# Third pair's second product by Strassen's scheme, with the weight sums made in place and the first product's weight sums read back from DRAM

## The chip, the cores and the metric

The kernel runs on one core of one Trainium2 chip. The metric is the device time of one launch in microseconds (us), lower is better. TensorE is called PE (matmuls) and PEld (weight loads), VectorE is DVE, ScalarE is ACT, GpSimd is POOL, SyncE is SP.

## The reference

Attention without softmax, and then a feed-forward block with a residual, for 8 batches of 448 rows, 12 heads of 64 columns (d_model 768), and d_ff 3072:

```python
scores = (q @ k.T) / sqrt(64)                 # per batch and head, 448 x 448
x = (maximum(scores, 0) ** 2 / 448) @ v       # heads side by side: 448 x 768
xn = (x - mean(x)) / sqrt(var(x) + 1e-6) * g_ln
out = x + maximum(xn @ w_ch1, 0) @ w_ch2      # 768 -> 3072 -> 768
```

The arrays are float32 in DRAM; the kernel multiplies in bfloat16 and sums in float32.

## The kernel before

**Pairs and stages.** The kernel works on pairs of batches: pair p holds batches 2p and 2p + 1, 896 rows. `xT[p]` is the attention's output with its columns on the partitions, `hT[p]` the hidden layer (24 row blocks of 128 x 896), `xtok[p]` the attention's output with tokens on the partitions, made from `xT[p]` by a DMA transpose (`tokens`). Pair 0 runs first, its pieces interleaved. After that, pairs are staggered, and each pass of the loop `for pair in range(pairs - 1)` runs two stages:

- A0, A1, A2: the second product (`hT[p]` times `w2`, L693) of pair 0, 1, 2, interleaved with the attention of the next pair (`attention`, L336 for scores, L368 for values).
- F1, F2, F3: the first product (`xT` times `w1`) of pair 1, 2, 3, in `ffn1_pair`.

The last part of the kernel is the second product of pair 3, with nothing beside it.

**Order.** The schedule is manual: each engine runs its instructions in the order in which the Python code issues them, and waits on semaphores for data or for a buffer to be free. Nothing reorders them. `interleave` spreads a list of side units evenly among a list of main units.

**Attention beside the second product.** A pair's attention has six groups of heads, n = 6p to 6p + 5, each with seven score tiles (128 x 896: two PSUM banks, three such tiles in turn, shared with the value product). Three score tiles form a bundle: 12 matmuls, three relus on ACT (L347), three squares on DVE (L351; in A0 the third on ACT, L349). Some bundles also hold a value product (28 matmuls, `product`), whose result DVE scales into `xT` (L374). A2 has 14 bundles, two hooks and a last value product: 17 side units. Keys and queries are loaded by POOL (`load`) and transposed by DMAs that SP issues (`transposed`, three groups ahead).

**The ordinary second product.** `ffn2` computes 128 tokens x 384 columns in 24 matmuls, in four units of six; two PSUM banks (`ps_mm`) alternate. DVE's L704 scales the result, adds the residual and so empties the bank. 14 such results make a pair: 336 matmuls. Rows 11 and 23 of `hT` come last (`late_rows`), because the last step of the stage before (`close`) makes them.

**Strassen's scheme for the first product.** `ffn1_pair` splits `w1` into four blocks, and the batch pair into two. For each of 12 iterations n it makes seven products of three matmuls instead of eight, on sums of blocks: products 3, 4, 1, then `close` of the iteration before (7 and 6), then 5 and 2. DVE adds the results: `z += b` (L863), `z += c` (L865), `a = z - a` (L877), `b = z - b` (L880). Product 2 accumulates into bank b, so it can't start before L863 has read that bank. The sums of `w1` blocks are made by POOL and DVE, in F2 they are also stored to `kept` in DRAM (`keep`, 44 stores on SP), and in F3 they are read from there (`given`). The sums of `xT` halves (L738) are made in `even`, `odd` and `start`.

**Strassen's scheme for the last pair's second product.** `ffn2_pair` takes token tiles t and t + 4 together (t = 0, 1, 2) and both column halves, four results, with seven products of 12 matmuls, 84 instead of 96. The left sides are sums of `hT` blocks (s1, s2, s5, s6, s7; `h_sums_of`, L942 to L948), the right sides blocks of `w2` (t2, t5) or their sums (t1, t3, t4, t6, t7). POOL makes t3, t4, t1 and t6 in F3 (48 instructions, L923), DVE t7 after it, all into buffers of their own. In the four results, `d`, `c12`, `c21` and `q_` are float32 buffers in SBUF; ACT copies banks into them, DVE and POOL add them up. Token tile 3 is left to `ffn2`.

Of the kernel before, what the change touches and what calls it, by code (L numbers as in the profile page):

```python
# [28 lines left out]
def kernel(  # L29
# [54 lines left out]
    xcpool = ctx.enter_context(tc.tile_pool(name="xc", bufs=2))  # L84
    xtpool = ctx.enter_context(tc.tile_pool(name="xt", bufs=1))
    hpool = ctx.enter_context(tc.tile_pool(name="h", bufs=1))
    opool = ctx.enter_context(tc.tile_pool(name="o", bufs=3))
# [8 lines left out]
    eps_sb = const.tile([P, 1], fp32)  # L96
    nc.vector.memset(eps_sb, 1e-6)
    ones = const.tile([P, P], bf16)
    nc.vector.memset(ones, 1.0)


# [16 lines left out]
    def load(n, names):  # L118
        if n >= len(groups):
            return  # L120
        b, m = groups[n]
        for name in names:
            if b == 1 and name != "v":
                o = (2 * m + "qk".index(name)) * 2 * S
                t = hold[:, o:o + 2 * S].rearrange("p (r s) -> p r s", r=2)
            elif name == "q":
                t = qbuf[m][:, D:D + 2 * S].rearrange("p (r s) -> p r s", r=2)
            else:
                t = io.tile([P, 2, S], bf16, tag=name, name=name + "_sb", bufs=4 if name == "v" else 3)
            nc.gpsimd.dma_start(t, srcs[name][b][:, m:NP:G, :])  # L130
            qkv[name, b, m] = t
# [34 lines left out]
    qkv["k", 0, 0] = io.tile([P, 2, S], bf16, tag="k", name="k_sb", bufs=3)  # L166
# [62 lines left out]
    def transposes(b, m):  # L229
# [8 lines left out]
        else:  # L238
            sb = tpool.tile([P, NB, P], bf16, tag="qT", name="qT_sb", bufs=3)
# [41 lines left out]
    def keys_dma(n):  # L281
        kts[n] = tpool.tile([P, J, P], bf16, tag="kT", name="kT_sb", bufs=3)
        nc.sync.dma_start_transpose(kts[n], qkv[("k",) + groups[n]].rearrange("p r s -> p (r s)"))

    def queries_dma(n):
        m, kt = groups[n][1], kts[n]
        qt = tpool.tile([P, NB, P], bf16, tag="qT", name="qT_sb", bufs=3)
# [69 lines left out]
    def values(n, blk):  # L357
# [21 lines left out]
        if b not in xc:  # L379
            xc[b] = xcpool.tile([P, K1, S + 2], bf16, tag="xc", name="xc_sb")  # L380
# [35 lines left out]
    def fold_tiles():  # L416

        t = xcpool.tile([P, K1, S + 2], bf16, tag="xc", name="fold_sb").rearrange("p c s -> p (c s)")
# [54 lines left out]
    def transposed(n):  # L473
# [6 lines left out]
        if n > by_dma * G:  # L480
            load(n + 2, "kq")
        keys_dma(n)
        queries_dma(n)

# [77 lines left out]
    def attention(bs, hooks):  # L562
# [9 lines left out]
        def item(n, i, act):  # L572
            scores(n, (i,), FULL, act)
            if i == J - 1 and n + 3 < len(groups):
                transposed(n + 3)

        def product(n):
            values(n, FULL)
            load(n + 4, "v")
# [120 lines left out]
    def finish(pair, t, half, lo, hi, ps, queues):  # L700

        cols, w = slice(half * DH + lo * D, half * DH + hi * D), (hi - lo) * D
        o = opool.tile([P, DH], fp32, tag="o", name="o_sb")
# [18 lines left out]
    def ffn1_pair(pair, keep=False, prepare=None, between=None):  # L722
# [6 lines left out]
        xd = xcpool.tile([P, K1, S + 2], bf16, tag="xc", name="x_sum")[:, :, :S]  # L729
# [3 lines left out]
        rooms[0] = {m: room0[:, a:b] for m, (a, b) in kinds.items()}  # L733
        given = prepare is not None

        def x_sum(m, a, b, op):
            if given:
# [9 lines left out]
        def sums_early(n):  # L747
# [5 lines left out]
            if given:  # L753
                queue = nc.scalar if n > 2 else nc.sync
                queue.dma_start(w[n]["early"], kept[:, n, :3 * KQ])
# [8 lines left out]
        def sums_late(n):  # L764
            if n >= KH:
                return
            if given:
                nc.sync.dma_start(w[n]["late"], kept[:, n, 3 * KQ:])
# [43 lines left out]
        def even():  # L812
            if given:
                rooms[0].update(early=room0[:, :3 * KQ], late=room0[:, 3 * KQ:])
            sums_early(0)
            nc.vector.tensor_add(x[5], lo[:, :KQ], lo[:, KQ:])
            sums_late(0)
            sums_last(0)

        def odd():  # L820
            nc.vector.tensor_sub(x[6], hi[:, :KQ], lo[:, :KQ])

        def start():
            z = xcpool.tile([P, K1, S + 2], bf16, tag="xc", name="z_sb").rearrange("p c s -> p (c s)")
            temps.extend(z[:, i * S2:(i + 1) * S2].bitcast(fp32) for i in range(2))
            if given:
                room, pool = prepare()
                for i, m in enumerate((1, 2, 7)):
                    x[m] = room[:, i * KQ * S:(i + 1) * KQ * S].rearrange("p (c s) -> p c s", s=S)
                for i in range(1, 3):  # L830
                    t = pool.tile([P, 5 * KQ, P], bf16, name=f"w1_room{i}")
                    rooms[i] = {m: t[:, a:b] for m, (a, b) in kinds.items()}
                    rooms[i].update(early=t[:, :3 * KQ], late=t[:, 3 * KQ:])
                for n in (1, 2):
                    sums_early(n)
                    sums_late(n)
            else:
# [3 lines left out]
                for i in range(1, 3):  # L841
                    one, two = (apool.tile([P, 2, 512], bf16, tag="attn", name="w1_sum")
                                .rearrange("p r (c n) -> p (r c) n", n=P) for _ in range(2))
                    rooms[i] = {3: two[:, :3], "4a": one[:, 6:8], "4b": two[:, 6],
                                4: (None, one[:, 6], one[:, 7], two[:, 6]),
                                1: one[:, :3], 6: one[:, 3:6], 7: two[:, 3:6], "16": one[:, :6]}
            x_sum(1, lo[:, :KQ], hi[:, KQ:], nc.vector.tensor_add)
            x_sum(2, hi[:, :KQ], hi[:, KQ:], nc.vector.tensor_add)
            x_sum(7, lo[:, KQ:], hi[:, KQ:], nc.vector.tensor_sub)
            if not given:  # L850
# [41 lines left out]
    w2_sum, h_sum, h_sums = {}, {}, (("s2", "s5"), ("s1",), ("s6",), ("s7",))  # L892
# [5 lines left out]
    def late_pools():  # L898

        late = ctx.enter_context(tc.tile_pool(name="late", bufs=1, side="right"))  # L900
        for name in ("t1", "t3", "t4", "t6"):
            w2_sum[name] = late.tile([P, KH, DH], bf16, name="w2_sum_" + name)
        w2_sum["t2"], w2_sum["t5"] = w2_part(0, 0), w2_part(1, 1)
        last = stage_sums.enter_context(tc.tile_pool(name="x_sums", bufs=1, side="right"))
        w1_pool = stage_sums.enter_context(tc.tile_pool(name="w1_kept", bufs=1, side="right"))
        return last.tile([P, KH * DH], bf16, name="x_sum"), w1_pool

    def late_pools_two():

        two = ctx.enter_context(tc.tile_pool(name="late2", bufs=1, side="right"))  # L910
        w2_sum["t7"] = two.tile([P, KH, DH], bf16, name="w2_sum_t7")
        return two

    def w2_sum_units():

        b = {(i, j): w2_part(i, j) for i in range(2) for j in range(2)}
        pairs = (("t3", (0, 1), (1, 1)), ("t4", (1, 0), (0, 0)), ("t1", (0, 0), (1, 1)),
                 ("t6", (0, 0), (0, 1)), ("t7", (1, 0), (1, 1)))

        def unit(name, x, y, i, n):  # L920
            engine = nc.vector if name == "t7" else nc.gpsimd
            op = engine.tensor_sub if name in ("t3", "t4") else engine.tensor_add
            op(w2_sum[name][:, i:i + n], b[x][:, i:i + n], b[y][:, i:i + n])  # L923
        return [lambda name=name, x=x, y=y, i=i, n=n: unit(name, x, y, i, n)
                for name, x, y in pairs for n in ((3,) if name == "t7" else (1,)) for i in range(0, KH, n)]

    def h_sum_tiles():

        three = xpool.tile([P, 3, KH, P], bf16, tag="xT", name="h_sum")
        h_sum["s2"], h_sum["s5"], h_sum["s1"] = (three[:, i] for i in range(3))  # L930
        h_sum["s25"] = three[:, 0:2]
        for name in ("s6", "s7"):
            t = xcpool.tile([P, K1, S + 2], bf16, tag="xc", name="h_sum1").rearrange("p c s -> p (c s)")
            h_sum[name] = t[:, :KH * P].rearrange("p (k s) -> p k s", s=P)

    def h_sums_of(pair, t, names, lo, hi):
# [300 lines left out]
```

## Time and profile before

| | us |
|---|---|
| median of three runs | 521.63 |
| profiled execution | 522.39 |
| its span, first to last instruction | 520.6 |
| start: pair 0 up to its hidden layer | 0 to 99.0 |
| A0 | 99.0 to 175.6 |
| F1 | 175.6 to 222.2 |
| A1 | 222.2 to 297.4 |
| F2 | 297.4 to 344.0 |
| A2 | 344.0 to 416.2 |
| F3, with the last 18 matmuls of A2's product | 416.2 to 466.4 |
| second product of pair 3, and the tail | 466.4 to 520.6 |

PE is busy for 511.9 us of the span at a granted clock of 0.999. The lines that the prediction shows are of four kinds: the page's head; busy time by stretch; the chain of work that ended last; and the timeline, where each line has the start, the length, the engine, the source line, the operation, what it writes and reads, and how many instructions of one kind were merged. A bracket at the end tells how long the engine was idle before it, and for whom. Source lines are those of the kernel before; where the text speaks of an instruction that only the changed kernel has, the line is one of the changed kernel (L739 is its L704, L380 its L351, L1118 and above are in `ffn2_pair`).

### The profile page before, as it was taken

What the parts mean: (1) busy time and instruction counts of PE and PEld (TensorE: products, weight loads), DVE (VectorE), ACT (ScalarE), POOL (GpSimd) and SP (SyncE); (2) the same over time, 40 slices, a digit from 0 to 9 for tenths busy, and PEclk for the clock granted to TensorE, in tenths of its full rate; (3) what the DMA queues carried; (4) which work ended last, traced back from release to release, by engine and by line L of the source; (5) the groups of instructions that cost most, each with busy time, mean ns of one, the idle gap of its engine ahead of it and who ended that gap; (6) DMA issues with size and microseconds to landing.
All of it is one profiled execution on the core that took longest, in us unless ns stands there. A gap on an engine that the chain in (4) does not pass through costs nothing.

```text
span 520.6 us, 11553 instructions
## 1 busy us (share of the span) xinstructions
PE 511.9 (98%) x4601; PEld 303.8 (58%) x4601; DVE 381.2 (73%) x734; ACT 300.6 (58%) x492; POOL 163.0 (31%) x213
## 2 busy tenths in 40 slices
PE   8999999999999999999999999999999999999996
PEld 6677778855555555555555555555555554555663
DVE  5875665399899798756777688857676678866773
ACT  6967675498768276656646266656646446751110
POOL 7335102112311375101222166500000049970331
PEclk9999999999999999999999999999999999999999
DMA  9999999999969920217999995514762195411123
GB/s 197 206 206 207 210 199 167 163 156 161 193 121 170 185 48 0 37 25 131 188 182 153 177 205 175 150 54 94 130 95 69 44 203 173 131 39 30 42 54 88
DMA packets 120936, 68.46 MB, mean 132 GB/s; under 512 B 79410, under 2 KB 118834, under 8 KB 120882
## 3 DMA queue, kind: packets, MB, share of 16 engines
q1 hardware_dynamic: 91746, 38.72, 37.1%
q0 software_dynamic: 26976, 25.50, 32.9%
q10 hardware_dynamic: 2160, 3.51, 2.3%
q8 instruction: 36, 0.59, 0.5%
q14 instruction: 18, 0.15, 0.1%
HBM read 57.81 MB, written 16.91 MB: 144 GB/s over the span
## 4 chain that ended last, share of the span: by engine, by line
PE 89%; DMA 7%; DVE 1%; POOL 1%; issue 1%; ACT 0%; SPq 0%; POOLq 0%
PE o_ps L693 33%; PE m_ps L796 25%; PE m_ps L963 8%; PE h_ps L634 7%; PE sc_ps L336 7%; PE av_ps L368 6%; DMA w<-in_moe_w_ch_dram 3%; DMA xtok_sb<-xT_sb 2%; PE h_ps L678 2%; DMA v_sb<-in_v_dram 2%; PE h_ps L660 1%; PE tr_ps L221 1%; PE sum_ps L401 0%; ACT attn_sb L347 0%; DVE x_sum L738 0%
## 5 line engine op out<-in xcount | busy, mean ns | idle before, releaser
L693 PE MATMUL o_ps<-w,hT_sb 128*128 128x384 bf16 x1056 | 181.7, 326 | 0.0
L347 ACT ACTIVATE attn_sb<-sc_ps 128x896 bf16<-128x896 f32 (+4 forms) x150 | 126.4, 902 | 64.7 <-PE sc_ps L336 56.1
L693 PEld LDWEIGHTS <-hT_sb 128*128 128x128 bf16 x1056 | 99.3, 98 | 76.9 <-issue 15.2
L800 ACT ACTIVATE hT_sb<-m_ps 128x448 bf16<-128x448 f32 x144 | 78.2, 544 | 47.0 <-PE m_ps L796 44.6
L351 DVE TENSOR_TENSOR attn_sb<-attn_sb 128x896 bf16<-128x896 bf16 x112 | 71.8, 650 | 38.1 <-ACT attn_sb L347 37.5
L130 POOL DMA_DIRECT2D v_sb<-in_v_dram x24 | 17.2, 716 | 162.7 <-PE sc_ps L336 131.3
L923 POOL TENSOR_TENSOR w_sum_t<-w 128x384 bf16<-128x384 bf16 x48 | 41.8, 903 | 50.8 <-DVE w_sum_t L1141 50.8
L796 PE MATMUL m_ps<-x_sum,w 128*128 128x448 bf16 x216 | 47.0, 352 | 0.5 <-DVE z_sb L863 0.5
L634 PE MATMUL h_ps<-xc_sb,w 128*128 128x256 bf16 (+2 forms) x384 | 43.8, 263 | 0.5 <-DMA w<-in_moe_w_ch_dram 0.5
L634 PEld LDWEIGHTS <-w 128*128 128x128 bf16 x384 | 33.8, 97 | 7.3 <-issue 2.9
L877 DVE TENSOR_TENSOR m_ps<-z_sb,m_ps 128x448 f32<-128x448 f32 x36 | 22.6, 628 | 20.3 <-ACT hT_sb L800 20.0
L796 PEld LDWEIGHTS <-w_sum 128*128 128x128 bf16 x240 | 23.5, 98 | 21.8
L374 DVE TENSOR_SCALAR xT_sb<-av_ps 128x896 bf16<-128x896 f32 (+2 forms) x30 | 27.0, 900 | 12.2 <-PE av_ps L368 12.0
L336 PE MATMUL sc_ps<-qT_sb,kT_sb 64*64 64x448 bf16 x504 | 35.3, 358 | 0.0
L861 ACT COPY z_sb<-m_ps 128x448 f32<-128x448 f32 x36 | 19.2, 533 | 26.6 <-PE m_ps L796 25.8
L796 PEld LDWEIGHTS <-w 128*128 128x128 bf16 x216 | 21.1, 98 | 20.5 <-issue 0.7
L368 PE MATMUL av_ps<-attn_sb,v_sb 64*64 64x448 bf16 (+2 forms) x672 | 32.4, 327 | 0.1
L704 DVE SCALAR_TENSOR_TENSOR o_sb<-o_ps,rstd_sb,xtok_sb 128x384 f32<-128x384 f32 x44 | 26.9, 611 | 5.9 <-PE o_ps L693 5.5
L796 PE MATMUL m_ps<-x_sum,w_sum 128*128 128x448 bf16 x144 | 31.2, 352 | 0.0
L368 PEld LDWEIGHTS <-v_sb 64*64 64x64 bf16 x840 | 23.1, 107 | 11.2 <-issue 2.2
L611 DVE BATCH_NORM_STATS2 stats<-xtok_sb 128x6 f32<-128x384 bf16 x56 | 28.3, 548 | 0.8 <-DMA xtok_sb<-xT_sb 0.8
L644 ACT ACTIVATE hT_sb<-h_ps 128x256 bf16<-128x256 f32 (+1 forms) x49 | 18.1, 368 | 16.0 <-PE h_ps L634 15.1
(149 smaller groups left out, 693.2 us busy)
## 6 DMA issues: line engine op xcount, KB each, us to landing
out_dram<-o_sb SPq DMA_DIRECT2D x90, 96.0 KB, 2.3
v_sb<-in_v_dram POOLq DMA_DIRECT2D x24, 224.0 KB, 5.1
w<-in_moe_w_ch_dram POOLq DMA_DIRECT2D x12, 384.0 KB, 14.4
w<-in_moe_w_ch_dram POOLq DMA_DIRECT2D x4, 1152.0 KB, 20.0
q_sb<-in_q_dram POOLq DMA_DIRECT2D x20, 224.0 KB, 5.6
k_sb<-in_k_dram POOLq DMA_DIRECT2D x20, 224.0 KB, 5.5
kept<-room SPq DMA_DIRECT2D x4, 480.0 KB, 3.1
w_room<-kept ACTq DMA_DIRECT2D x6, 288.0 KB, 3.2
```

The lines of the kernel that those rows point to most:

```text
L336: nc.tensor.matmul(ps[cols, r, o * w:(o + 1) * w], g["k"](i)[rows, cols], g["q"](i, r)[rows, blk[0]:sum(blk), cols], start=True, stop=True)
L347: nc.scalar.activation(a, ps[:, :, :len(slots) * w], ACTF.Relu)
L351: nc.vector.tensor_mul(a, a, a)
L368: nc.tensor.matmul(ps[cols, hh, :w], v_sb[rows, pr, j * D:(j + 1) * D], g["attn"][i][rows, r, :], start=(j == 0), stop=(j == J - 1))
L374: nc.vector.tensor_scalar_mul(x, ps[:, :, :w], score_scale)
L611: nc.vector.bn_stats(stats[:, n], xtok[pair][:, n * G:(n + 1) * G, t, :])
L634: nc.tensor.matmul(ps[:, :w + more], w1[:, c, ni * P:(ni + 1) * P], xc[b][:, c, s.start:s.stop + more], start=(c == 0), stop=(c == K1 - 1))
L693: nc.tensor.matmul(ps[:, :DH], hT[pair][:, ki, t * P:(t + 1) * P], w2[:, ki, cols], start=(o == 0), stop=(o == K2 - 1))
L796: nc.tensor.matmul(ps, *at, start=(first and c == 0), stop=(c == KQ - 1), skip_group_check=not first)
L800: nc.scalar.activation(hT[pair][:, n + KH * row, half * S:(half + 1) * S], ps, ACTF.Relu)
L923: op(w2_sum[name][:, i:i + n], b[x][:, i:i + n], b[y][:, i:i + n])
L963: nc.tensor.matmul(ps, x[:, ki], y[:, ki], start=(first and ki == 0), stop=(ki == KH - 1), skip_group_check=not first)
```

## The change

The second product of pair 2 (in A2) is made as that of pair 3 is: three times `ffn2_pair`, and token tile 3 by a new `ffn2_mid`, with as many matmuls as before. Both are generators now, so that they can be cut into units of about six matmuls. What follows from it:

- Pair 2's `ffn2_pair` has only the two banks of `ps_mm`, because the attention has the other six. Pair 3's has six, as before.
- The `w2` sums must be there before A2. t3 and t4 are made in place, in blocks of `w2` (POOL, 24 instructions in F2, behind a `gate`), t7 in a spare buffer (DVE, after iterations 1, 2 and 3 of F2), t1 and t6 in quarters of `w1` that F2 and F3 don't read (DVE, six instructions in A1).
- F1 stores the `w1` sums to `kept`, and F2 and F3 both read them (`keep=pair == 0`, `given=pair > 0`).
- The left sums s6 and s7 are made in place in `hT`.
- Buffers for q, k, v and their transposes are fixed slots now, some of them in the spare buffer until t7 needs it; after that there is one slot fewer, transposes are issued two groups ahead and the loads of q and k behind them.
- In A2, ACT squares the third score tile of each bundle, as in A0.
- In F3 all five sums of `xT` are made in `start`, ahead of the last five units of A2's second product; before it was three, ahead of the last three units.
- The statistics of pair 2's tokens are made during F2 (from iteration 3 on) and not beside A2.

```diff
     def item(n, i, act):
         scores(n, (i,), FULL, act)
-        if i == J - 1 and n + 3 < len(groups):
-            transposed(n + 3)
+        ahead = 3 if n + 3 < LATE else 2
+        if i == J - 1 and n + ahead < len(groups) and (ahead == 3 or n + 2 >= LATE):
+            transposed(n + ahead)
...
-                item(*it, o == 2 and bs[0] == by_dma)
+                item(*it, o == 2 and bs[0] in (by_dma, B - 2))
...
         def start():
...
+            if given:
+                for n in (1, 2):
+                    sums_early(n)
+                    sums_late(n)
             x_sum(1, lo[:, :KQ], hi[:, KQ:], nc.vector.tensor_add)
+            if wide_x:
+                x_sum(5, lo[:, :KQ], lo[:, KQ:], nc.vector.tensor_add)
             x_sum(2, hi[:, :KQ], hi[:, KQ:], nc.vector.tensor_add)
             x_sum(7, lo[:, KQ:], hi[:, KQ:], nc.vector.tensor_sub)
+            if wide_x:
+                x_sum(6, hi[:, :KQ], lo[:, :KQ], nc.vector.tensor_sub)
...
+    def w2_sum_tiles():
+        for name, (i, j) in (("t2", (0, 0)), ("t5", (1, 1)), ("t3", (0, 1)), ("t4", (1, 0))):
+            w2_sum[name] = w2_part(i, j)
+        for name, c, o in (("t1", 0, KH * P), ("t6", KQ, 0)):
+            w2_sum[name] = [w1[:, c + k // 4, o + k % 4 * DH:o + (k % 4 + 1) * DH] for k in range(KH)]
+        w2_sum["t7"] = spare.rearrange("p (k n) -> p k n", n=DH)
...
         if "s6" in names:
-            nc.vector.tensor_sub(h_sum["s6"][:, lo:hi], a[1, 0], a[0, 0])
+            nc.vector.tensor_sub(a[1, 0], a[1, 0], a[0, 0])
...
+    def ffn2_mid(pair, a, b):
+        h = hT[pair].rearrange("p (kh k) s -> p kh k s", kh=2)[:, :, :, 3 * P:4 * P]
+        s, n = room0[:, :KH], KH - 1
...
+        yield from most(a, h[:, 1], "t4", first=True)
+        nc.vector.tensor_add(s[:, :n], h[:, 0, :n], h[:, 1, :n])
+        yield
+        yield from most(b, h[:, 0], "t3", first=True)
+        yield
+        nc.vector.tensor_add(s[:, n], h[:, 0, n], h[:, 1, n])
+        for names in (("s2", "s5"), ("s1",), ("s6",), ("s7",)):
+            h_sums_of(pair, 0, names)
+        yield from most(a, s, "t2")
+        yield
+        yield from most(b, s, "t5")
+        yield
...
+        for half, ps in enumerate((a, b)):
+            finish(pair, 3, half, 0, K1, ps, (nc.sync, nc.sync))
...
+    def between_two(n):
+        if n == 0:
+            side.update(gps=w2_sum_units("t3") + w2_sum_units("t4"), t7=w2_sum_units("t7"),
+                        tokens=token_units(2)[1:])
+            nc.vector.memset(gate[:, :1], 0.0)
+            nc.gpsimd.tensor_copy(gate[:, 1:], gate[:, :1])
+        if 0 < n <= KQ:
+            side["t7"].pop(0)()
+        for _ in range(2):
+            side["gps"].pop(0)()
+        if n > 2 and side["tokens"]:
+            side["tokens"].pop(0)()
...
+        return [lambda: next(g)] * 4, [lambda: next(g)] * (5 + 3 * 14), g
...
-        units = ffn2_units(pair)
+        if last:
+            mm = [ps_mm.tile([P, 512], fp32, tag="mm", name="o_ps") for _ in range(2)]
+            outs += [x_room.rearrange("p b c s -> p (b c s)")[:, 3 * KH * P:3 * KH * P + 2 * DH].bitcast(fp32),
+                     room0[:, 9:].rearrange("p c n -> p (c n)").bitcast(fp32)]
+            h_sum_tiles()
+            head, units, _ = strassen_units(pair, mm, lambda t: mm[::-1] if t % 2 else mm)
+        else:
+            units = ffn2_units(pair)
+            head, units = (units[:2], units[2:]) if pair else ([], units)
...
+        if pair == 1:
+            w2_sum_tiles()
+            sums = w2_sum_units("t1") + w2_sum_units("t6")
+            units = beside_of(units, {8 + 6 * n: f for n, f in enumerate(sums)})
...
-        interleave(units[:-3], beside)
+        few = 5 if last else 3
+        interleave(units[:-few], beside)
...
         hook("start")
         ps_m = open_narrow()
-        for unit in units[-3:]:
+        for unit in units[-few:]:
             unit()
```

So A2 has four units as its head before `close`, 42 main units among the 17 side units, and five units after them. A unit is half a product, six matmuls; the first five main units are the rest of `ffn2_mid` (26 matmuls), and each of the three tiles has 14. Within a tile the products come in the order 3 (bank a), 2 (b), 5 (a, accumulating on 3), 4 (b, on 2), 1 (a), 6 (b), 7 (a, on 1). Between them stand, on ACT, the copy of a into `d` after 3, of a into `c12` after 5 (L1133) and of b into `c21` after 4; on DVE, `d -= b` after 2 (L1130), `q_ = a + d` after 1 (L1141), `q_ += b` after 6 (L1146), then the next tile's s6, `c12` and `c21` scaled onto the residual (L1118), `d` likewise (L1152), and after 7 the sum of `d` and a (L1155); on POOL, `d - c12 + c21` after 1 and the residual of `q_` after 6.

More of the change, by code (lines that the diff above doesn't have):

```diff
@@ L890, in ffn1_pair @@
         return dict(even=even, odd=odd, start=start, run=run, close=close)
-    w2_sum, h_sum, h_sums = {}, {}, (("s2", "s5"), ("s1",), ("s6",), ("s7",))
+    w2_sum, h_sum = {}, {}
     def w2_part(n, half):
         return w2[:, n * KH:(n + 1) * KH, half * DH:(half + 1) * DH]
[L898 to L906, printed above, removed]
@@ L1187, with banks @@
     pair = pairs - 1
[L1188 to L1190 removed]
+    z = late[0].tile([P, 5, DH], fp32, tag="z", name="z_sb")
+    outs[3:] = [z[:, i] for i in range(5)]
+    mm = [ps_mm.tile([P, 512], fp32, tag="mm", name="o_ps") for _ in range(2)]
+    def banks(t):
+        return [ps_m.tile([P, 512], fp32, tag="m", name="m_ps") for _ in range(2)]
+    head, _, rest = strassen_units(pair, mm, banks)
+    for unit in head:
         unit()
     stage["close"]()
[L1193 to L1206 removed]
+    for _ in rest:
+        pass
 _INS = ['q', 'k', 'v', 'moe_g_ln', 'moe_w_ch1', 'moe_w_ch2']
```

296 lines of the change are left out of this document (171 added, 125 removed).

## The prediction

> **What bounds the kernel now.** First the page's head and its engine table, then busy time by stretch, for the stretches named in the section on the profile: A0, F2, A2, F3.
>
> ```profile
> span 520.6 us, 11553 instructions
> ...
> PE 511.9 (98%) x4601; PEld 303.8 (58%) x4601; DVE 381.2 (73%) x734; ACT 300.6 (58%) x492; POOL 163.0 (31%) x213
> ```
> ```profile
> 99.00:175.60 76.60, 76.42 (x701) 42.14 (x699) 68.33 (x125) 54.52 (x72) 16.09 (x22) 1.00 1.05 163
> ...
> 297.40:344.00 46.60, 46.60 (x249) 24.05 (x247) 39.07 (x73) 30.87 (x57) 24.11 (x32) 1.00 0.63 163
> 344.00:416.20 72.20, 72.20 (x661) 39.11 (x660) 48.77 (x92) 38.81 (x52) 1.43 (x2) 1.00 0.41 79
> 416.20:466.40 50.20, 49.75 (x266) 25.86 (x266) 39.20 (x74) 30.96 (x58) 41.80 (x48) 1.00 0.56 143
> ```
>
> After the stretch and its length come busy PE, PEld, DVE, ACT and POOL. From 99 us on PE never rests, apart from 0.45 us in F3 and the tail: a matmul taken away is time gained, and a wait of PE is time lost one for one. So I count PE's matmuls and PE's new waits; the rest matters only where it makes PE wait.
>
> **What is removed.** A2's second product takes 48 + 3 x 84 = 300 matmuls instead of 336. The chain of waits prices one by the same arithmetic at the end of the kernel:
>
> ```profile
> 475.32 40.96 PE m_ps L963 x252
> ```
> 0.1625 us each, and 36 x 0.1625 = **-5.85 us**.
>
> **What is moved or added at no cost.** The 44 stores to `kept` move on SP from F2 to F1. F2 has them now and takes 46.6 us, F1 has none and takes 46.6 us: free. F2 reads `kept` as F3 does now (12 early parts, nine of them issued from ACT at about 0.35 us, and 12 late ones from SP); F3 ran so with ACT at 31 of 50 us. A1 gets six DVE sums of 1536 elements (L948 takes 0.95 us for that many) and loses one pair of `w1` sums; DVE rests for 22 of A1's 75 us. With that cover gone it would be 5 us; I take 0. POOL's 48 sums in F3 go; PE waited for none of them, so 0. The last pair's four DVE sums (2.75 us) go too, beside PE; 0. The head before `close` grows from 12 to 22 matmuls of the same total.
>
> **F2: three DVE sums for t7.** They stand behind iterations n = 1, 2, 3, and n = 3 also has a statistic. The timeline of one iteration:
>
> ```profile
> 304.07 1.30 PE L796 MATMUL m_ps<-xT_sb,w_sum 128*128 128x448 bf16 x6
> ...
> 304.85 0.63 DVE L880 TENSOR_TENSOR m_ps<-z_sb,m_ps 128x448 f32<-128x448 f32 x1
> ...
> 305.94 0.61 DVE L863 TENSOR_TENSOR z_sb<-z_sb,m_ps 128x448 f32<-128x448 f32 x1
> ...
> 306.91 1.30 PE L796 MATMUL m_ps<-x_sum,w 128*128 128x448 bf16 x6
> ```
>
> From the iteration's start at T = 304.07, DVE is through L880 at T + 1.41. PE's product 2 is the second half of the group at 306.91, at T + 3.41, and needs L863 (0.61). So 1.39 us of other DVE work fit between. A t7 sum beside POOL's 24 back-to-back sums takes between 0.95 us (L948) and 1.75:
>
> ```profile
> 487.46 1.00 POOL L1046 TENSOR_TENSOR z_sb<-z_sb 128x384 f32<-128x384 f32 x1
> 487.53 1.75 DVE L946 TENSOR_TENSOR h_sum<-hT_sb 128x1536 bf16<-128x1536 bf16 x1
> ...
> 488.42 1.63 POOL L1025 TENSOR_TENSOR z_sb<-z_sb,xtok_sb 128x384 f32<-128x384 f32 x1
> ...
> 489.20 1.80 DVE L1021 SCALAR_TENSOR_TENSOR z_sb<-z_sb,rstd_sb,xtok_sb 128x384 f32<-128x384 f32 x2
> ```
>
> With two bf16 statistics and their aggregate (1.19 us) n = 3 overruns by 0.75 to 1.55 us, and n = 1, 2 by 0 to 0.35 each: 0.75 to 2.25. In between, at 1.3 a sum (L772, 0.55 us alone, is 0.70 in F2's mean with POOL half busy), only n = 3 waits: **+1.1**.
>
> [...]
>
> **A2: opening.** After `close` (end E): two relus 0.6 us, the small row of s 0.2, four h sums 4.36 (L942 to L948, 470.08 to 474.44 now), two squares 1.1, and only then DVE's L739 (0.61) empties bank a: E + 6.9. PE has 26 matmuls and two bundles in front of product 3 of the first tile, which writes that bank: 4.2 + 2 x 0.8 = E + 5.8. **+1.05**, between 0 and 1.1.
>
> **A2: middle.** ACT gets the square of every third score tile, plus four fp32 passes per tile (0.48 x 3 + 0.62):
>
> ```profile
> 146.82 2.53 ACT L347 ACTIVATE attn_sb<-sc_ps 128x896 bf16<-128x896 f32 x3 [2.77 <-PE sc_ps L336]
> 149.38 0.95 ACT L349 ACTIVATE attn_sb<-attn_sb 128x896 bf16<-128x896 bf16 x1
> ```
>
> A bundle is 3.5 us of ACT. Seventeen side units beside 42 main units put bundles behind main units 3, 5, 8, 10, 13, 15, 18, 20, 23, 28, 30, 33, 35, 38; six gaps are two units, 2 x 0.98 + 0.79 = 2.75 us, less than 3.5. Where such a gap ends in a bundle with a value product, its third score tile reuses a PSUM buffer whose relu comes late: twice 0.5 us by my walk through the queues. DVE has 9 to 10 us per tile beside squares and scalings of 8, in about 20 of PE. Its burst at a tile's end (q 0.55, s6 0.95 to 1.75, the two L1118 1.8, L1152 0.6) holds the squares that the value products of bundles 7, 10 and 12 need: 0.3 + 0.1 + 1.25. The last c12 copy stands behind bundle 13's relus: 0.65. Sum **+3.3**, between 0.5 (one buffer wait) and 6 (1 us at each short gap). In it too: transposes two groups ahead instead of three, behind a bundle about 7.6 us before its scores are due; A2's three issues now span 2.7 us and land 3.2 to 4.6 later, 6 to 7.5. And on POOL the last loads of q and k now wait for the transposes that empty their buffers, the first tile's two passes stand behind them, and DVE's L1118 behind those: up to 1 us more, inside the bounds.
>
> **A2: end.** The timeline:
>
> ```profile
> 414.65 1.52 PE L368 MATMUL av_ps<-attn_sb,v_sb 64*64 64x448 bf16 x28
> ...
> 416.11 3.10 PE L693 MATMUL o_ps<-w,hT_sb 128*128 128x384 bf16 x18
> 416.23 1.09 DVE L374 TENSOR_SCALAR xT_sb<-av_ps 128x896 bf16<-128x896 f32 x1 [1.82 <-PE av_ps L368]
> ...
> 417.35 2.40 DVE L738 TENSOR_TENSOR x_sum<-xT_sb 128x1344 bf16<-128x1344 bf16 x3
> ...
> 419.04 1.30 PE L796 MATMUL m_ps<-xT_sb,room 128*128 128x448 bf16 x6
> ```
>
> Now three x sums hide behind 18 matmuls. Afterwards five are queued on DVE (2.40 for three, so 3.9 for five) ahead of `q_ = a + d` of the last tile (L1141, 0.56), and product 7 accumulates into the bank that this reads. PE has 18 matmuls (2.9 us) before product 7; DVE needs 1.1 + 3.9 + 0.56 and reaches it 5.65 us after the value product. **+2.7**. Behind it POOL's two passes (2.6) hold L1118 and L1155, so the first `z` sum of F3 is some 0.6 late for its product 2; the 0.45 us wait for xtok in F3 should vanish as DVE gets there later. **+0.15**, between 0 and 0.6.
>
> **Sum.** -5.85 + 1.1 + 1.05 + 3.3 + 2.7 + 0.15 = +2.45. The profiled execution (522.39 us, 1.8 outside its span) becomes 524.8; it lies 0.76 above the median of the three runs, 521.63, so I say **524.1 us**. With the terms at their bounds: -5.85 + 0.75 + 0 + 0.5 + 2.6 + 0 = -2.0 and -5.85 + 2.25 + 1.1 + 6 + 2.9 + 0.6 = +7.0: 519.6 to 528.6.
>
> **Rivals.** *The gain comes through.* PE ran A0 with DVE at 68.3 of 76.6 us and waited 0.2; if queues absorb all but the x sums, it is -5.85 + 2.7, 518.5, and 515.8 if these hide too. Against it: in A0 no product waited for a bank that DVE or ACT had just to read; here two banks carry seven products a tile. *ACT sets A2's pace.* A2 gets 42 x 0.85 + 14 x 0.95 + 3 x 2.1 = 55 us of ACT in about 66. If each of 14 bundles makes PE wait 1 us, the middle costs 14 instead of 3.3: 534.8. It passes 2% (10.4 us) from 11.3 us, 0.8 per bundle. For it: 3.5 against 2.75. Against it: the seven other gaps are 3.7 us and more. *Late transposes.* If the two that are due after 7.6 us land as slowly as A0's worst (7.7 after their issue, instead of 4.6), 3 us at two places: 530.
>
> **Chances.** Forecast 0.57, the gain comes through 0.25, ACT's pace 0.10, late transposes 0.08. The range 517 to 530 leaves out about 0.2. A change of 2% is about what a measurement of this kernel can tell from none; faster by that needs more than the removed matmuls, 0.01; slower needs ACT's pace in earnest, 0.07; within, 0.92.
>
> **What would show it.** PE's idle time by releaser: in A2 waits for L739, for squares (L380) at the value products, and one of 2 to 3 us for L1141; in F2 one of about 1 us for the z sum of n = 4. PE matmuls of A2's second product: 300. F1 and A1 as long as before, F3 without waits on DMA. Wrong if A2's waits are below 4 us or above 12, or if PE waits in F1, A1 or the last pair.

## The result, and the profile after

The changed kernel takes 543.93 us (median of six runs, 541.15 to 545.95) against 522.52 us for the kernel before on the same chip: a ratio of 1.0407, 95% interval 1.0367 to 1.0447. It is slower by 4%, and the time lies outside the predicted range. One execution of the kernel before took 1848.64 us, and one each of the experiments e6_late_act and e7_layout was over 1.5% above its run's fastest: the ratios, and the medians of these two runs, leave them out. The profiled execution took 543.38 us, its span is 540.2. First the page's head and engine table:

```profile
span 540.2 us, 11478 instructions
...
PE 512.4 (95%) x4565; PEld 301.3 (56%) x4565; DVE 386.1 (71%) x718; ACT 316.7 (59%) x512; POOL 129.7 (24%) x167
```

PE has 36 fewer matmuls to do and is busy as long as before (511.9), though idle for 27.8 us instead of 8.7. Where it idles is told by PE's waits by releaser, from A0 to the end (total, times, longest):

```profile
PE m_ps L847 <- DVE x_room L924: 7.0, 1, 7.0
PE m_ps L847 <- DMA w_sum<-kept: 4.2, 2, 2.3
PE o_ps L1061 <- DVE o_room L1141: 2.7, 1, 2.7
PE o_ps L1061 <- ACT o_room L1133: 2.0, 2, 1.4
PE sc_ps L365 <- ACT attn_sb L376: 0.9, 4, 0.3
PE m_ps L847 <- DMA room<-kept: 0.9, 1, 0.9
PE o_ps L1061 <- DVE room L739: 0.6, 1, 0.6
```

Each stage's length, from the first matmul of one stage to that of the next in PE's timeline (the head of A2 counts to A2), in us:

| | F2 | A2 | F3 | last pair |
|---|---|---|---|---|
| before | 46.56 | 75.22 | 47.18 | 54.38 |
| after | 52.35 | 80.17 | 56.23 | 54.43 |
| difference | +5.79 | +4.95 | +9.05 | +0.05 |
| predicted | +1.1 | +1.2 | +0.15 | 0 |

F2 starts 0.24 us earlier than before, so F1 and A1 took nothing. A2 and F3 by busy time (PE, PEld, DVE, ACT, POOL, granted clock, DMA share, GB/s):

```profile
349.50:429.70 80.20, 72.84 (x644) 38.27 (x642) 56.27 (x76) 55.05 (x72) 14.77 (x16) 0.99 0.54 100
429.70:485.90 56.20, 49.22 (x248) 24.73 (x246) 37.39 (x71) 30.91 (x58) 0.38 (x1) 0.93 0.56 118
```

The granted clock of F3 (third column from the end) was 1.00 before and is 0.93. Cut finer, the loss of clock stands in two stretches, behind the waits of 2.7 and 7.0 us:

```profile
427.80:431.20 3.40, 3.40 (x12) 1.53 (x11) 3.23 (x4) 0.49 (x2) 2.20 (x3) 0.50 0.00 0
...
451.70:455.10 3.40, 3.40 (x10) 1.36 (x10) 2.76 (x5) 1.08 (x2) 0.00 (x0) 0.50 0.28 73
```

For 3.4 us each the granted clock was 0.50 and PE busy throughout, so each cost 1.7 us on top of the wait itself: the nine matmuls behind the 7.0 us took 3.31 us up to the next one's start, nine of the same shape at the start of F2 took 1.70. Below, such a stretch is called a half clock.

**F2.** The waits for `kept` are 0.92, 1.88 and 2.35 us, together 5.15 of the 5.79. SP's timeline, the first line before the change, the others after it:

```profile
299.90 6.31 SPq L604 DMA_TRANSPOSE xtok_sb<-xT_sb  x1
...
299.66 12.46 SPq L639 DMA_TRANSPOSE xtok_sb<-xT_sb  x1
312.22 0.52 SPq L783 DMA_DIRECT2D room<-kept  x1
312.85 0.86 SPq L783 DMA_DIRECT2D w_sum<-kept  x2
```

Issuing one transpose held SP for 12.46 us (6.31 before), and the reads behind it went out only at 312; the wait of 2.35 us is for one of these. The early parts, issued from ACT at 300.12 and 304.10, were not held by SP, and yet landed 8.8 and 10.9 us later; the other two waits, 2.80 us together, are for them. So two causes are possible: SP's queue, or the DMA engines that transpose and reads share (while the transpose ran, 299.6 to 318, the time of SP's packets adds up to 88% of the 16 engines' span and that of ACT's to 28%).

**F3.** The chain of waits around the 7.0 us:

```profile
435.15 14.72 DMA xtok_sb<-xT_sb
449.89 1.03 DVE stats L646 x2
...
451.07 0.59 DVE x_room L924
```

SP's timeline ahead of the transpose, before and then after:

```profile
420.30 1.11 SPq L715 DMA_DIRECT2D out_dram<-o_sb  x2
421.46 7.47 SPq L604 DMA_TRANSPOSE xtok_sb<-xT_sb  x1
...
430.11 3.69 SPq L750 DMA_DIRECT2D out_dram<-o_room  x6
433.90 1.21 SPq L750 DMA_DIRECT2D out_dram<-room  x2
435.15 7.72 SPq L639 DMA_TRANSPOSE xtok_sb<-xT_sb  x1
```

xtok's transpose went out 5.6 us after the stage's first matmul (429.54) instead of 2.4, because eight stores of A2's last tile stood ahead of it on SP (4.9 us of issuing) where there were two before (1.1 us), and they waited for the last passes of POOL and DVE. It also took 14.7 us to land instead of 10.6; why, no run settles. DVE took the first statistic behind n = 2, stood there, and the `z` addition behind it on DVE (L924) stood too.

**A2.** Its named waits are 0.6 (L739), 2.0 (L1133) and 2.7 us (L1141), and 0.9 us of the half clock falls before n = 0. The rest is small change in attention: PE's busy time and idle time for scores and values together is 11.6 + 9.0 = 20.6 us before and 12.6 + 1.1 + 10.0 + 1.0 = 24.7 after. -5.85 + 0.6 + 2.0 + 2.7 + 0.9 + 4.1 = +4.45 of the +4.95; the other 0.5 isn't traced.

### The profile page after: what moved, and what is told of

It is laid out like the page before. It is cut to its first block, busy times and chain, and to the rows that moved or that the text cites. A ratio compares the mean times of both kernels' runs of the same rounds, so it can differ in the third digit from the quotient of the medians.

```text
span 540.2 us, 11478 instructions
## 1 busy us (share of the span) xinstructions
PE 512.4 (95%) x4565; PEld 301.3 (56%) x4565; DVE 386.1 (71%) x718; ACT 316.7 (59%) x512; POOL 129.7 (24%) x167
## 4 chain that ended last, share of the span: by engine, by line
PE 81%; DMA 6%; ACT 6%; DVE 4%; issue 2%; SPq 0%; ACTq 0%; DVEq 0%
PE m_ps L847 23%; PE o_ps L728 20%; PE m_ps L1061 8%; PE h_ps L669 7%; PE sc_ps L365 6%; PE av_ps L397 5%; ACT attn_sb L376 4%; PE o_ps L1061 3%; DMA xtok_sb<-xT_sb 3%; PE o_ps L1017 3%; PE h_ps L713 2%; DMA room<-kept 2%; PE h_ps L695 1%; ACT early L376 1%; DMA w_sum<-kept 1%
## 5 line engine op out<-in xcount | busy, mean ns | idle before, releaser
L728 PE MATMUL o_ps<-w,hT_sb 128*128 128x384 bf16 x672 | 116.0, 326 | 0.0
L728 PEld LDWEIGHTS <-hT_sb 128*128 128x128 bf16 x672 | 63.0, 98 | 48.8 <-issue 10.1
L380 DVE TENSOR_TENSOR attn_sb<-attn_sb 128x896 bf16<-128x896 bf16 x98 | 61.3, 637 | 30.6 <-ACT attn_sb L376 30.0
L669 PE MATMUL h_ps<-x_room,w 128*128 128x256 bf16 (+2 forms) x384 | 43.8, 263 | 0.4 <-ACT early L376 0.3
L1061 PEld LDWEIGHTS <-hT_sb 128*128 128x128 bf16 x288 | 28.0, 98 | 23.3 <-issue 5.6
L847 PE MATMUL m_ps<-x_sum,w 128*128 128x448 bf16 x144 | 33.9, 357 | 7.0 <-DVE x_room L924 7.0
L938 DVE TENSOR_TENSOR m_ps<-x_room,m_ps 128x448 f32<-128x448 f32 x36 | 22.6, 629 | 22.8 <-ACT hT_sb L851 22.5
L159 POOL DMA_DIRECT2D k_sb<-in_k_dram x15 | 10.7, 712 | 100.5 <-DMA kT_sb<-k_sb 79.8
L922 ACT COPY x_room<-m_ps 128x448 f32<-128x448 f32 x36 | 19.1, 532 | 24.6 <-PE m_ps L847 24.0
L1061 PEld LDWEIGHTS <-x_room 128*128 128x128 bf16 x216 | 20.5, 98 | 18.0 <-issue 5.2
L378 ACT ACTIVATE attn_sb<-attn_sb 128x896 bf16<-128x896 bf16 x28 | 26.6, 950 | 0.9
## 6 DMA issues: line engine op xcount, KB each, us to landing
w<-in_moe_w_ch_dram POOLq DMA_DIRECT2D x12, 384.0 KB, 13.9
```

Of the source, the lines that this page charges most:

```text
L378: nc.scalar.activation(a, a, ACTF.Square)
L380: nc.vector.tensor_mul(a, a, a)
L669: nc.tensor.matmul(ps[:, :w + more], w1[:, c, ni * P:(ni + 1) * P], xc[b][:, c, s.start:s.stop + more], start=(c == 0), stop=(c == K1 - 1))
L728: nc.tensor.matmul(ps[:, :DH], hT[pair][:, ki, t * P:(t + 1) * P], w2[:, ki, cols], start=(o == 0), stop=(o == K2 - 1))
L847: nc.tensor.matmul(ps, *at, start=(first and c == 0), stop=(c == KQ - 1), skip_group_check=not first)
L1061: nc.tensor.matmul(ps, x[:, ki], y[ki] if isinstance(y, list) else y[:, ki], start=(first and ki == 0), stop=(ki == KH - 1), skip_group_ch ...
```

## The experiments

Three questions: what makes the reads of F2 late, whether A2's end, the late transpose and the half clock are one chain, and what eats A2's saving. Medians of each run, with stage lengths of its profiled execution (these vary: with the waits for `kept` different each time, the executions of one run spread by up to 1.1%; F2, which e1_stats and e2_xsums leave as it is, took 56.72 and 51.97 us there):

| run | median us | ratio to before (95%) | F2 | A2 | F3 | last |
|---|---|---|---|---|---|---|
| e1_stats | 539.70 | 1.0291-1.0391 | 56.72 | 80.03 | 52.49 | 54.40 |
| e2_xsums | 534.43 | 1.0189-1.0274 | 51.97 | 76.55 | 52.38 | 54.44 |
| e3_tok2 | 543.26 | 1.0369-1.0423 | 54.20 | 80.58 | 54.42 | 54.41 |
| e6_late_act | 544.02 | 1.0365-1.0425 | 57.25 | 79.35 | 54.36 | 54.38 |
| e7_layout | 539.89 | 1.0236-1.0393 | 50.30 | 81.20 | 54.25 | 55.20 |
| e8_split | 539.13 | 1.0302-1.0333 | 49.78 | 81.26 | 53.99 | 54.10 |
| e9_all | 534.83 | 1.0195-1.0282 | 47.11 | 75.26 | 51.89 | 60.89 |
| e10_all_dve | 534.57 | 1.0218-1.0253 | 47.12 | 77.64 | 51.89 | 59.74 |
| e11_plain | 528.74 | 1.0092-1.0133 | 54.67 | 75.23 | 48.21 | 54.46 |
| e12_all2 | 526.77 | 1.0055-1.0111 | 48.66 | 75.52 | 51.08 | 54.35 |
| e13_all2_alt | 527.17 | 1.0055-1.0110 | 46.86 | 76.47 | 51.04 | 54.33 |
| e14_no_hsums | 526.78 | 1.0056-1.0108 | 47.12 | 74.98 | 51.08 | 54.28 |

The last four are within 2% of the kernel before, though each interval lies above 1. The code of each is shown shortened.

### F2: late parts from another queue

```diff
-                fetch(nc.sync, n, "late")
+                fetch(nc.sync if wide_x or n < 3 else nc.scalar, n, "late")
```

> Edit: in F2 the late parts of kept for n=3 and on are issued on ACT's queue instead of SP's (where the transpose of xtok stands ahead of them for 12.5 us), nothing else. Theory A (the hold of SP's queue is what costs): the wait for the late part of n=4 (2.35 us) goes, those for the early parts (0.92 and 1.88) stay: -2.3 us, 541.6. Rival B (the transpose takes the DMA engines, whatever queue a read is on): the late parts land late all the same and the early parts behind them on ACT's queue later still: 3.5 to 6 us of waits in F2, 543 to 546.

544.02 us: no gain. PE's waits in F2:

```profile
PE m_ps L847 <- DVE x_room L924: 5.3, 1, 5.3
PE m_ps L847 <- DMA w_sum<-kept: 2.9, 1, 2.9
PE m_ps L847 <- DMA room<-kept: 0.3, 1, 0.3
```

The late part's wait of 2.35 us is gone, as theory A says: that one was SP's hold. But reads that stand behind the transpose in no queue still cost 3.2 us (2.8 before the edit), and the transpose itself is later: it landed 22.8 us after its issue, its statistic waited, and 5.3 us came up at L924. The time is rival B's: transpose and reads were slow beside one another, on either queue. In the changed kernel the reads that ACT issued from 304 to 313 landed 6.9 to 10.9 us later, and those from 325 to 334, behind the transpose, 2.7 to 3.1 us later; the transpose took 18.2 us there and 8.3 in F2 before, beside stores alone. While the changed kernel's transpose ran (299.6 to 318), the DMA engines were busy for nine tenths and more in 34 of 40 slices, which fits a shortage of engines; no run separates them from what else the transfers share.

### F2: the transpose later, or in parts

```diff
 # e3_tok2: between_two; the statistics then two a unit from n = 6
+        if n == 3:
+            tokens(2)
 # e8_split: between_two, with the same statistics
+        if n < K1:
+            nc.sync.dma_start_transpose(xtok[2][:, n], xT[2][:, n, :])
```

> Edit: in F2 the transpose of xtok is issued behind n=3 instead of ahead of n=0, and its statistics run two a unit behind n=6 to n=9, nothing else. Theory A (the transpose and the reads of kept share the DMA engines and SP's queue, wherever they meet): the three waits of n=3 and n=4 (5.15 us) go, but reads that are now beside the transpose come late for n=6 and n=7, 2 to 5 us: total 541 to 544 us. Rival B (only the crowd at the start of F2 is too much: two units' reads, v, the last stores and the transpose at once): all three waits go and none comes: 538.7 us, F2 47.2 us instead of 52.35.

> Edit: in F2 the one transpose of xtok is issued as six, one of each 128x896 block behind each of n=0 to n=5, with the statistics two a unit from n=6, nothing else. Theory A (the price is that one transpose holds SP's queue for 12.5 us and the DMA engines for 18 us at a stretch): each sixth holds SP for about 1.5 to 2 us, the reads land within 3 to 6 us as F3's did before, PE's waits for kept in F2 fall from 5.15 us to under 1: 539 us. Rival B (the reads are late for their own sake, their tiles or their size): the waits stay, 543 to 545 us. Rival C (each transpose costs a fixed time that six pay six times): DMA busier, waits in n=2 to n=6, 544 to 548 us.

Moved whole (543.26 us), the waits for `kept` move too: 2.5 + 1.8 us, where 5.15 was, and two statistics a unit cost 1.3 us. As theory A said, it cost where it met the reads, 4.3 us there. In six parts (539.13 us) F2 has no wait for `kept` at all, as its theory A said; PE's longest waits there:

```profile
PE m_ps L851 <- DVE x_room L928: 2.0, 3, 0.7
```

These are three units with two statistics each, 0.67 us apiece. Each part held SP for 1.2 to 1.35 us and landed in 4.3 to 7.0. With one statistic a unit (e9_all, e13_all2_alt) F2 takes 47.11 and 46.86 us, 0.3 to 0.5 over before: the same reads, from the same queues into the same buffers, cost nothing there. (Not every execution is so: that of e12_all2, with the same F2, still waited 1.7 us for `kept`.)

### F2: where the parts are cut

```diff
-  "early": [(one, 0)], "late": [(two[:, :7], 8)]}
+  "early": [(one, 0), (two[:, :1], 8)], "late": [(two[:, 1:7], 9)]}
```

> Edit: in F2, for the iterations whose sums of w1 lie in attention's buffers, the third block of product 1 is read with the early part (one read more on ACT's queue) and not with the late part, nothing else. In those buffers the late part is otherwise due in its iteration's product 1, one iteration sooner than in F3, where it is first used by close. Theory A (that is what F2 has and F3 had not): the wait inside n=4's product 1 (2.35 us of the 5.15) goes and the others stay, F2 50 us instead of 52.35, 541.5 in all. Rival B (the DMA engines are short beside the transpose, however the reads are cut): the waits sum to 4 to 6 us as before, 543 to 545.

539.89 us and F2 50.30: near theory A's numbers, but not by its mechanism. PE's waits in F2:

```profile
PE m_ps L847 <- DMA room<-kept: 2.5, 2, 2.4
PE m_ps L847 <- DMA w_sum<-kept: 0.6, 1, 0.6
```

The wait inside n = 4's product 1 is gone, but 2.36 us were waited in `close` instead, for the late part that SP issued at 311.54, behind the transpose: as much as before (2.35). What fell is the waits for the early parts, to 0.17 and 0.57 from 0.92 and 1.88, and theory A had these staying. They also differ from one execution of the same F2 to another (2.6 us together in e2_xsums, 4.25 in e1_stats), so this run doesn't show that the cut of the parts matters. It shows SP's hold once more.

### F3 and the end of A2

```diff
 # e1_stats: between_three
-        if n > 1 and side["tokens"]:
+        if n > 3 and side["tokens"]:
 # e2_xsums: start() keeps x sums 1 and 5; 2, 7 and 6 go here:
         for unit in units[-few:]:
             unit()
+        if last:
+            following["rest"]()      # the x sums 2, 7 and 6
```

> Edit: in F3 the token statistics of the last pair start two units later (behind n=4 instead of n=2), nothing else. Theory A (DVE in order: a statistic that waits for xtok holds the z additions behind it, and PE stands until DVE comes to them): the wait at L847 for x_room L924 falls from 7.0 us to at most 0.6, the granted clock stays 1.00 in F3, which gives back another 1.7 us (3.4 us at 0.50), so F3 falls from 56.2 us to 47.5-48.5 and the whole by 8 to 8.7 us: 535.5 us against 543.9. Rival B (F3 is short of what DRAM sends, and the stall only covered it: two reads of kept landed 9.1 us after their issue there): waits of PE for w_room<-kept come up, 2 to 5 us in all, and the time is 537 to 541 us.

> Edit: of the five x sums ahead of A2's last units, three (for products 2, 7 and 6) are issued behind these units, nothing else. Theory A (the 2.66 us wait at L1141 is DVE's queue, and the half clock that follows is the idle PE's price): the wait goes, the clock stays 1.00 at the start of F3 (4.4 us together), and since the results of the last tile are no longer late on DVE, the last stores leave SP some 3 us sooner after n=0 begins, the transpose of xtok goes out sooner, and the 7.0 us wait in F3 falls to 3 to 4 us: -8 us, 536 us. Rival B (SP's transpose is held by other things, the F3 wait stays 7): -4.4 us, 539.5. Rival C (the sums that were moved are then late themselves in F3, each 0.8 us of DVE ahead of the z additions): only -2 us, 542.

e1_stats gained 4.2 us, half of theory A's 8.0 to 8.7. The 7.0 us wait is gone from F3, but PE then waited 3.2 us there for `w_room<-kept`, followed by 3.3 us at a granted clock of 0.50: rival B's range. The stall had covered reads that were late beside the transpose. (F2 fell badly in that execution: 6.3 us of waits and two half clocks, 3.3 and 3.2 us at 0.50.) e2_xsums gained 9.5: A2 is 3.6 us shorter, and F3 3.85. L1141's wait fell to 0.3, and the half clock behind it went. F3's gain isn't what theory A meant, though. The transpose went out 6.4 us after n = 0's first matmul, later than the 5.6 of the changed kernel: the eight stores stand ahead of it as before, wherever the x sums are (rival B's premise). It landed in 11.7 us instead of 14.7, which no edit explains. And 3.5 us came up at L928 (this kernel's `z += b`), behind the moved sums, which is rival C's wait; it held PE back, so that only 0.6 us were left for the statistic. In F3 3.5 + 0.6 + 1.4 us of waits and half clock (nine matmuls in 3.06 us instead of 1.70) stand where 7.0 + 1.7 + 0.8 stood.

### All of them together

Both runs have the transpose in parts in F2 and F3 with statistics one a unit from n = 5, the x sums moved, and, in A2, fixed out buffers:

```diff
-        d = fp()
+        d = fp(3 + t % 2)
...
-        c12 = fp()
+        c12 = fp(0)
```

> Edit, three together: in F2 and F3 the transpose of xtok goes out in six parts (two behind n=0, one behind each of n=1 to n=4) with one statistic a unit from n=5; three of the five x sums behind A2's last units; and fixed float32 out buffers in A2, so that the copy of c12 of a tile never takes the buffer whose store left last. Theory A (each wait has its own cause, and they add): F2 loses its 5.15 us of waits for kept, A2's end 2.66 us and the half clock behind it 1.7, F3 its 7.0 us and 1.7, the copy of c12 1.4 to 2.0: 543.9 - 20 = 524 us (523 to 526), what is left being A2's middle, the 0.6 of L739 and 1 to 1.5 of DVE in F2. Rival B (the stall in F3 comes back as another, since the late stores still hold SP): F3 keeps 3 to 5 us, 527 to 530.

534.83 us, 10 more than expected. F2, A2 and the c12 copy did as theory A said; two waits are new:

```profile
PE m_ps L1071 <- ACT o_room L1095: 3.6, 1, 3.6
PE m_ps L853 <- DVE x_room L934: 3.5, 1, 3.5
```

Both are of the experiment's making. The three x sums stood ahead of n = 0's additions (L934), and the fixed buffers, which reached the last pair too, made its last tile wait for a store (L1095). Each was followed by a half clock: nine matmuls in 3.29 us instead of 1.70 behind the 3.5, 24 in 6.73 instead of 3.90 behind the 3.6. With the transpose in parts F3 has no wait for it, nor for `kept`. e12_all2 mends both:

> Edit: the three edits together again, but mended in two places where the run with them lost time anew: the x sum for product 2 is issued behind the z additions of n=0 and those for 7 and 6 at the end of n=0 (not all ahead of n=0's z additions), and the fixed out buffers hold for A2 alone, the last pair taking its own in turn as in the changed kernel. Theory A (each wait with its own cause, and each idle stretch of PE of about 3 us costs another 1.7 us of half clock): the 3.51 us ahead of n=0's product 5 and the 3.60 us in the last pair go with their half clocks, 10.4 us: 534.8 - 10.4 = 524.4 us (523 to 526), F2 0.5 over before, A2 and F3 within 1 of before. Rival B (DVE has too much to do around the start of F3, wherever it stands): 2 to 4 us come back in n=0 or n=1, 527 to 529.

526.77 us, ratio 1.0083 (1.0055 to 1.0111): 2.4 more than theory A and at rival B's lower end. The last pair is as before again. F3 is 3.9 us longer than before, since DVE is short of time around n = 0:

```profile
PE m_ps L853 <- DVE x_sum L795: 2.7, 1, 2.7
```

With the half clock behind it (1.7: 18 matmuls in 5.08 us instead of 3.40) that is 4.4 us. From the last value product's scaling to the end of the x sums behind n = 0, 13.9 us, DVE rests for only 1.4. No version that I ran beats the kernel before.

### A2: where the saving went

```diff
 # e10_all_dve (on e9_all): no squares on ACT in A2
-                item(*it, o == 2 and bs[0] in (by_dma, B - 2))
+                item(*it, o == 2 and bs[0] == by_dma)
 # e13_all2_alt (on e12_all2): ACT's square in 8 bundles of 14, ... no in (1, 3, 5, 7, 8, 10, 12, 13)
 # e14_no_hsums (on e12_all2):
-            if t < 2:
+            if t < 2 and pair == pairs - 1:
                 h_sums_of(pair, t + 1, (name,))
 # e11_plain (on the changed kernel): head, units = ffn2_units(2) split as before, few = 3
```

> Edit: A2's product in the ordinary way (336 matmuls, no h sums, with three units and not five behind the attention), everything else as in the changed kernel; w2 holds sums by then, so this pair's output is another one, and only the time is meant. Theory A (most of the loss is not Strassen's in A2 but what was moved around it): F2 keeps its 52.3 us (+5.7), A2 is 72 to 73 us with no wait for L1141, L1133 or L739; xtok of the last pair goes out 3 us sooner after n=0, so F3's wait falls from 7.0 to 3 to 4 us: 530 to 532 us, that is still 9 us over before. Rival B (the loss is Strassen's): 522 to 525.

528.74 us, less than theory A's 530 to 532, and F3 is better than it said (waits of 1.4 in all): two stores, not eight, stand ahead of the transpose, which went out 4.0 us after the stage's first matmul and landed in 10.0. Its A2, in one stretch:

```profile
351.90:427.13 75.23, 75.23 (x680) 40.91 (x679) 33.93 (x52) 51.06 (x60) 5.05 (x7) 1.00 0.57 103
```

75.23 us without a wait, as before (75.22), though ACT has its 14 squares here too. F2, with nothing of Strassen's second product in it but the sums of `w2`, stays 8.1 us over before in this execution, the slowest of four. Of the 21.4 us, then, 6.3 by the medians (ratio 1.0113, 1.0092 to 1.0133) come with what was moved, and the other 15 need the schedule of A2: its own waits, its eight late stores, and what these set off in F3.

> Edit: as the run with the three edits together, and A2's squares are all on DVE again (in the changed kernel ACT takes one of three). Theory A (ACT sets the pace of A2's middle: 3.5 us a bundle against 2.55, and scores and values stand 4.1 us longer than before): 2 to 3 us less than that run, 521 to 522. Rival B (DVE is the bound, with its bursts at the ends of tiles): 14 squares of 0.64 us more on it, the wait at L380 grows from 0.6 to 2 or 3 us, and L1141 waits again: 1 to 3 us more than that run, 525 to 527.

> Edit: as that run, with ACT taking its square in 8 of A2's 14 bundles, those before the longer intervals (three units of the product and more), and DVE the others. Theory A (ACT is late only in the short intervals, two units): scores and values stand 4.1 us in all with ACT taking every bundle's, 2 or so with this: 1.5 to 2 us less than that run, 522 to 523, no faster than before by more than a measurement can tell. Rival B (the same work is short on either engine): within 0.7 us of that run.

> Edit: as the mended run with the three edits together (526.8 us), with A2's h sums for its second and third tile left out (DVE then has eight operations, some 9 us, less in A2; this pair's output is another one, and only the time is meant). In that run scores and values stand 3.9 us longer in A2 than before and the other waits of A2 are 1.6 us. Theory A (DVE's bursts at the ends of the tiles make the squares and so the values late): scores and values come down to within 1.5 us of before, A2 falls by 2.5 to 4 us, 523 to 524.5. Theory B (ACT's three exponentials and a square, 3.5 us a bundle, against two units of PE are the pace, whatever DVE does): scores and values stay over by 3 us or more, only the waits at the values' DVE steps and L1152 go, 525.5 to 526.5.

(ACT's "exponentials" in that text are its relus.) All three leave the time within 0.5 us of the run they start from. e13_all2_alt holds its rival B. e10_all_dve holds neither theory's time; in A2 it has rival B's waits for squares on DVE (1.7 instead of 0.6 us) and is 2.4 us longer there, where 108 matmuls of its product took 20.8 us, 1.2 more than in e12_all2. e14_no_hsums holds theory B in its stage, though its median gained nothing. Scores and values on PE (busy, mean ns | idle before, releaser), in e12_all2 and then in e14_no_hsums:

```profile
L367 PE MATMUL sc_ps<-qT_sb,kT_sb 64*64 64x448 bf16 x168 | 12.6, 359 | 1.1 <-ACT attn_sb L378 0.9 <-DVE xT_sb L405 0.2
L399 PE MATMUL av_ps<-attn_sb,v_sb 64*64 64x448 bf16 x168 | 10.0, 352 | 1.1 <-DVE attn_sb L382 0.6 <-ACT attn_sb L378 0.4
```
```profile
L367 PE MATMUL sc_ps<-qT_sb,kT_sb 64*64 64x448 bf16 x168 | 12.4, 360 | 1.8 <-ACT attn_sb L378 1.7
L399 PE MATMUL av_ps<-attn_sb,v_sb 64*64 64x448 bf16 x168 | 9.0, 350 | 0.4 <-ACT attn_sb L378 0.4
```

24.8 us with the h sums, 23.6 without, 20.6 before: 9 us less of DVE bring back 1.2 of 4.2; ACT's waits grow as DVE's go. Taking the squares from ACT instead (e10_all_dve) gives 12.7 + 0.2 + 10.4 + 2.5 = 25.8, with more of the waits on DVE. Relieving either engine alone doesn't bring the time back; both at once wasn't tried.

## Why the prediction was wrong

**"F2 reads `kept` as F3 does now: 0" failed: it measured 5.15 us.** I took F3's freedom from waits for a property of the reads, and looked at ACT's busy time. F3 before had them beside a transpose that landed in 10.6 us and held SP for 7.47; F2's took 18.2 and held SP for 12.46. Of the 5.15 us, 2.35 were for a read behind SP's hold (gone in e6_late_act) and 2.80 for reads from ACT's queue that landed late beside the transpose; in parts beside the same reads it cost nothing (e8_split). Why the whole transpose is so much slower in F2 than in F3 before, beside much the same reads, these runs don't settle. The row to read was SP's own timeline, where the transpose already held SP for 6.31 to 7.47 us with everything behind it.

**"A2 end: +2.7" was exact (2.66), what follows from it was left out.** The half clock after it costs 1.7, so a wait of PE is not "time lost one for one". And the term for F3 failed: "+0.15, the 0.45 us wait for xtok should vanish". It grew to 7.0, with another 1.7 of clock. I had followed the queue on DVE and not the one on SP: eight stores of the last tile, late for POOL's and DVE's passes, sent the transpose out 3.2 us later after the stage's start than before. With the ordinary product in A2 and two stores there (e11_plain), the longest wait in F3 is 1.0 us. The other half of the 7.0 is that the transpose took 4.2 us longer to land, and that cause stays open.

**A2's opening and middle (+4.35 together) were mis-sized.** Measured: 0.6 for the opening, 4.1 for scores and values and 2.0 for c12's copies, 6.7 in all; the middle's 6.1 is just over its upper bound of 6. Of the 2.0, 0.6 is the last copy behind ACT's relus, as predicted (0.65). The other 1.4 was not in the sum: the second tile's copy waited for the store of `d` of the tile before, whose buffer comes round five outs later, and that store stood on SP behind three transposes. With other buffers only the 0.6 is left (e12_all2). There A2 is 75.52 us, 0.3 over before; -5.85 + 4.2 + 1.6 makes 0.0 of it. Strassen's scheme gained its 36 matmuls and gave all of them back. The test that the prediction named, A2's waits between 4 and 12 us, was met (7.2): it looked at the stage where the smaller part was lost.

**t7's sums (+1.1)**, 1.58, 0.95 and 0.95 us long, cost 0.3 to 0.64 us; F1, A1 and the last pair cost nothing, as said. Of the rivals, "late transposes" named the right resource, but in A2 and for attention's tiles; there none was late.

## What to carry to other kernels

When a transfer is moved into a stage, lay it beside what is in flight there, and walk every in-order queue past which it goes to its end, SP's as well: here eight late stores sent F3's transpose out 5.6 us after the stage's start instead of 2.4. A long transpose was better issued in parts between the reads that are due (no wait for `kept` in F2 in e8_split, 5.15 us with it whole). And a saving on the busiest engine counted here only as far as the engines that feed it could follow its shorter interval (of 5.85 us of matmuls 4.2 went to scores and values in e12_all2, 1.6 to other waits): compare their work per interval, and not per stage.

## What the runs showed of the hardware

**A wait of PE cost more than itself.** In the changed kernel the granted clock was 0.50 for 3.40 us behind each of the waits of 2.66 and 6.98 us, in e1_stats for 3.2 to 3.3 us behind those of 4.25, 2.07 and 2.9 us. The matmuls show it as well: the 18 behind the 2.66 us took 4.77 us, 18 of the same shapes elsewhere 3.09. In PE's timelines from F2 on, of the changed kernel and the experiments, the matmuls behind eight waits of 3.08 us and more were 1.4 to 2.0 us slower in all, and 2.8 behind a ninth, the 3.60 us of e9_all. Of 16 waits between 2.0 and 3.0 us ten had a half clock behind them (one of 2.07 in e1_stats, 2.66 at L1141 in five traces) and six had not (2.15 to 2.48 in F2 in four traces, 2.66 and 2.92 in e6_late_act). A single long wait isn't needed: in A2 of e10_all_dve no wait was over 1.3 us, and yet 14 matmuls from 407.47 us on took 3.01 us, 14 of the same shape in e9_all 2.28. What sets the clock, these runs don't show.

**One transpose, 7.1 to 22.8 us.** `xtok` is 128 x 6 x 896 x 2 bytes, 1.38 MB. It landed in 8.3 us in F2 before, beside stores alone, in 10.6 beside the reads of F3, in 14.7 (F3) and 18.2 (F2) after the change, and in 22.8 in e6_late_act, with the late reads on ACT's queue too: 166 GB/s down to 60, counted from issue to landing. The fastest, 7.1 us in F1 before, is 194. Each of these had other transfers beside it; no run shows one alone.
